# Row-sum reciprocals and scalings moved to later steps in the 256-query blocks of a transformer layer, and one output product of the tail moved

## The chip, the cores and the metric

The kernel runs on one core of a Trainium2 chip. The metric is the device time of one launch in microseconds (us), the median of several runs. Lower is better.

## What is computed

A pre-norm transformer layer on one sequence of 2048 tokens with 512 features: attention with 32 heads of 16 features, and then a gated feed-forward part with 1792 inner features. Inputs are bf16.

```python
def _A_ref(x, wqkv, wo):                       # S=2048, D=512, H=32, Dh=16
    qkv = ((x @ wqkv).reshape(B, S, 3, H, Dh)).transpose(2, 0, 3, 1, 4)
    q, k, v = qkv[0], qkv[1], qkv[2]
    p = softmax(einsum("bhqd,bhkd->bhqk", q, k) * Dh ** -0.5)
    o = einsum("bhqk,bhkd->bhqd", p, v)
    return o.transpose(0, 2, 1, 3).reshape(B, S, D) @ wo
def _B_ref(x, w_gate, w_up, w_down):           # F=1792
    h = sigmoid(x @ w_gate) * (x @ w_up)
    return h @ w_down
h = x + _A_ref(_layernorm(x), A_wqkv, A_wo)
h2 = h + _B_ref(_layernorm(h), B_w_gate, B_w_up, B_w_down)
```

## The kernel before

**Tiling.** The queries are cut into five chunks (`CHUNKS`): three of 512 queries and, at the end, two of 256 (chunks 3 and 4). Within a chunk, the 32 heads are worked on in eight groups of four. One pair (chunk, head group) is called a block here and written (c, g). There are 39 blocks with a normalization of their own through DRAM, and 15 of these have 256 queries: (3, 0) to (3, 7) and (4, 0) to (4, 6). The last one, (4, 7), is normalized in the tail in another way.

**Steps.** Everything after a prologue is one list of 683 steps, written out by a loop over `i`. A step holds three score tiles of 128 keys by 512 columns. `emit_scores` writes the score products on TensorE (L937, with dummy products L914 at some steps) into one of two score buffers `pss`, and the exponentials of ScalarE (L948), which read them. At every fourth step (`i % 4 == 0`), and at a few more, the third tile is left to VectorE instead, which computes the exponential in pieces: `exp_bits` (L967) in the step itself, `exp_first` (L970 and L973) one step later, `exp_second` (L976) two steps later and `exp_third` (L980) three steps later. L967 is what reads the score buffer, so it sets it free for the scores two steps on.

The products with V (L1020, `emit_pv`) are planned by `plan_pv`: those of four steps are done six steps after the first of the four. With the last one of a block, at a step that I call the block's step i, `emit_norm` starts the normalization:

- VectorE copies the sums and unnormalized outputs out of `acc` (L993, `xs_all`). SyncE's queue (SP) writes the four rows of sums to DRAM (four issues, L996, `sd`) and reads them back spread over partitions (L997, `s_all`).
- `recip`, at a later step: VectorE's reciprocal (L1004, `r_all`), SP's write to DRAM (L1006, `rd`) and four broadcast reads (L1008, `rb_all`).
- `scale`, at a still later step: VectorE multiplies `xs_all` by `rb_all` into `OT` (L1000), which the output product reads (L630, `wo_mm`).

**Order in a step.** The engines run their instructions in the order in which the program writes them. A step is written in this order: the scores and exponentials with the loads of the Q rows of the next block (L246) and of its bounds (L256) on SP if they are due; the V products with `emit_norm`; what `later` put down for this step, in the order in which it was put down; and then the fill. The fill (`emit_fill`) takes work of other kinds from a generator: for the chunk before, the output product and layer norm (L630, L639, L147 to L158, transposes L164 and L165, loads of x with L635), the gate and up products (L655) with the tanh on ScalarE (L660) and the product on VectorE (`up_mul`, L668), and the down products (L671, L676, and the store L678). These products share one PSUM buffer `pm`: the next one can start only when the last one was read. At some steps the fill comes ahead of the V products or of what is due.

**The steps of a block's normalization.** A 256-query block ends at a step i with `i % 4 == 2`. Before the change, `recip` is due at i+6 and `scale` at i+11, except in (3, 7) and (4, 6), where they are due at i+5 and i+10.

**Tail.** `wo_early` writes the first output products of the last chunk's first 128 rows (head groups 0 to 6) as fill; the one of group 6 is held back until all steps are done. `ffn_last` then normalizes the last block with products on TensorE (L798 for the sums, L802, L805 and L806, L808), does the rest of the output products, and the feed-forward part of the last chunk.

Of the kernel before, what the change touches and what calls it, by code (L numbers as in the profile page):

```python
# [20 lines left out]
def kernel(  # L21
# [19 lines left out]
    NG = H // 4  # L41
    FC = F // P
    QC = 512
    TQ = QC // P
    CHUNKS = [(0, QC), (QC, QC), (2 * QC, QC), (3 * QC, QC // 2), (3 * QC + QC // 2, QC // 2)]
    NC = len(CHUNKS)
# [26 lines left out]
    def pm_tile():  # L73
        return pmh["pool"].tile([P, 512], FP32, name="pm")
# [424 lines left out]
    NS = len(groups)  # L499
# [124 lines left out]
    def tiles_of(c):  # L624
        q0, w = CHUNKS[c]
        return range(q0 // P, (q0 + w) // P)

    def wo_mm(ps, c, tt, g):
        assert ("o", c, g) in ready
        nc.tensor.matmul(ps[:], lhsT=OT[c % 2][:, g, tt * P:(tt + 1) * P], rhs=wo_pad[:, g, :],  # L630
                         start=(g == 0), stop=(g == NG - 1))

    def x_load(t):
        xr = pmh.get("work", work).tile([P, D], BF16, name="xr")
        nc.sync.dma_start(out=xr[:], in_=x_v[:, t, :])  # L635
        return xr
# [132 lines left out]
    def wo_early(c):  # L769
        early["x"] = [x_load(t) for t in tiles_of(c)]  # L770
        early[0] = pm_tile()
        for g in range(NG - 1):
            if g == NG - 2:
                for _ in range(3):
                    yield ("from", NS + LAG)
            yield 1
            wo_mm(early[0], c, 0, g)

    def ffn_last(c):
        q0, w = CHUNKS[c]  # L780
# [6 lines left out]
        def wo(tt, g0, g1):  # L787
            for g in range(g0, g1):
                wo_mm(pss[tt], c, tt, g)

        def add_x(tt):
            nc.tensor.matmul(pss[tt][:], lhsT=ident_bf[:], rhs=xrs[tt][:], start=False, stop=False)
# [16 lines left out]
                             rhs=ident_f[:], start=True, stop=True)  # L809
        nc.vector.tensor_tensor(out=OT[c % 2][:, NG - 1, 0:w], in0=xs, in1=rb[:, 0:w], op=ALU.mult)  # L810
        ready.add(("o", c, NG - 1))
        wo(1, 6, NG - 1)
        add_x(0)
        add_x(1)
# [57 lines left out]
    def filler():  # L872
        for t in range(NV0, NT):
            yield from fill_v(t)
        yield from fill_k(1, True)
        for b in range(2, 4):
            yield from fill_k(b)
            yield from fill_q0(b)
        for qc in range(1, NQC):
            yield from fill_q(qc)  # L880
        for c in range(NC - 1):
            yield ("from", int(first_step(c + 1)) + (11 if c + 3 >= NC else 15))
            yield from ffn_tasks(c)
        yield from wo_early(NC - 1)
# [98 lines left out]
    def norm_part(t, w, n):  # L983
        k = t.shape[1] * w // QC
        o = k * (n % (QC // w))
        return t[:, o:o + k]

    def emit_norm(c, g, i):
        w = CHUNKS[c][1]
        b = w // 32  # L990
        wait = int(w < QC and g < NG - 1 - (c == NC - 1))
        xs, rb, s32, r32 = (norm_part(t, w, g) for t in (xs_all, rb_all, s32_all, r32_all))
        nc.vector.tensor_copy(out=xs, in_=acc[:, 0:w])  # L993
        sd = dram.tile([4, w], FP32, name="sd", tag="sd%d" % w)
        for j in range(4):
            nc.sync.dma_start(out=sd[j:j + 1, :], in_=xs[32 * j + DH:32 * j + DH + 1, :])  # L996
        nc.sync.dma_start(out=s32, in_=sd[:].rearrange("j (a b) -> (j a) b", b=b))  # L997

        def scale():
            nc.vector.tensor_tensor(out=OT[c % 2][:, g, 0:w], in0=xs, in1=rb, op=ALU.mult)  # L1000
            ready.add(("o", c, g))

        def recip():
            nc.vector.reciprocal(out=r32, in_=s32)  # L1004
            rd = dram.tile([4, w], FP32, name="rd", tag="rd%d" % w)
            nc.sync.dma_start(out=rd[:].rearrange("j (a b) -> (j a) b", b=b), in_=r32)  # L1006
            for j in range(4):
                nc.sync.dma_start(out=rb[32 * j:32 * j + 32, :], in_=rd[j:j + 1, :].to_broadcast([32, w]))  # L1008
            later(i + 10 + wait, scale)
        later(i + 5 + wait, recip)  # L1010

    def emit_pv(c, g, k, i):
# [16 lines left out]
    def later(i, fn):  # L1029
        due.setdefault(i, []).append(fn)  # L1030

    p_of = {}
    fl = filler()
    state = {"turn": False, "wait": 0, "debt": 0.0, "done": False, "next": 0, "rate": None}

    def emit_fill(i):
        state["step"] = i
        r = rate(i)
        if not r or state["done"] or i < state["wait"]:
            state["debt"] = 0.0  # L1040
            return
        state["debt"] += state["rate"] or r
        while state["debt"] > 0 or isinstance(state["next"], tuple):
            c = state["next"]
            state["next"] = next(fl, None)
            if c is None:
                state["done"] = True
                return
            if isinstance(c, tuple):
                kind, n = c  # L1050
                if kind == "rate":
                    state["rate"] = n
                    continue
                state["debt"] = 0.0
                state["wait"] = i + 1 + n if kind == "gap" else i + 1 + (n - i - 1) % CYC if kind == "at" else n
                return
            state["debt"] -= c
            made[i] += c
# [11 lines left out]
    def load_w():  # L1070
        steps = [(wg[:, c, :], wg_v[:, c, :]) for c in range(DC)]
        steps += [(wu[:, c, :], wu_v[:, c, :]) for c in range(DC)]
        for k, (o, i) in enumerate(steps):
            later(44 + 5 * k, lambda o=o, i=i: nc.sync.dma_start(out=o, in_=i))
        for f in (0, 7):
            later(GM + 21 + f // 2, lambda f=f: nc.sync.dma_start(out=wd[:, f:f + 7, :], in_=wd_v[:, f:f + 7, :]))

    LAG = 2
# [10 lines left out]
    def plan_pv():  # L1089
        plan, last = {}, 0  # L1090
        for n, group in enumerate(groups):
            if n < G1:
                if n % CYC == 0:
                    last = n + CYC + 2
                    for k, u in enumerate(units[n * GU:(n + CYC) * GU:4]):
                        if k and u[2] == 0:
                            last += 1
                        plan.setdefault(last, []).append(u)
            else:
                for u in group:  # L1100
                    if u[3] == 3:
                        last = max(last, n + LAG)
                        plan.setdefault(last, []).append(u)
        return plan

    with tc.manual_schedule():
        p1ctx = ExitStack()
        pmh["pool"] = p1ctx.enter_context(tc.tile_pool(name="ps_p1", bufs=6, space=PSUM))
        prologue(p1ctx.enter_context(tc.tile_pool(name="pro", bufs=1)))
        p1ctx.close()  # L1110
        pmh["pool"] = ps_misc
        sctx = ExitStack()
        ps_s = sctx.enter_context(tc.tile_pool(name="ps_s", bufs=1, space=PSUM))
        ptp = sctx.enter_context(tc.tile_pool(name="ptp", bufs=1))
        pss2 = [ps_s.tile([P, GU, QC], FP32, name=f"pss{k}") for k in range(2)]
        pt4 = [ptp.tile([P, GU, QC], BF16, name=f"pt{k}") for k in range(4)]
        later(12, clear_wo)
        later(72, load_wo)
        later(90, lambda: nc.gpsimd.tensor_copy(out=ident_f[:], in_=ident_bf[:]))
        load_w()  # L1120
        pv_due = plan_pv()
        n_pv = {i: len(us) if i < G1 + CYC else 0 for i, us in pv_due.items()}
        for i in range(NS + LAG):
            if i < NS:
                emit_scores(i)
            if i == NS + LAG - 1:
                while next(fl) == 1:
                    pass
            us = pv_due.pop(i, [])
            early_fill = i >= 2 * CYC and any(u[2] == 0 for u in us)  # L1130
            for u in us:
                if early_fill and u[2] == 0:
                    emit_fill(i)
                emit_pv(*u[:3], i)
            if state["turn"] and i == state["wait"] and not early_fill:
                emit_fill(i)
                early_fill = True
            for fn in due.pop(i, []):
                fn()
            if 1 <= i < NS and not early_fill:  # L1140
                emit_fill(i)
        for _ in fl:
            pass
        sctx.close()
        pmh["pool"] = ctx.enter_context(tc.tile_pool(name="ps_t", bufs=6, space=PSUM))
        pmh["work"] = ctx.enter_context(tc.tile_pool(name="tail", bufs=4))
        assert not due
        ffn_last(NC - 1)


# [28 lines left out]
```

## Time and profile before

| | us |
|---|---|
| median of 3 runs | 951.39 |
| lowest and highest of these | 951.03 and 952.76 |
| the profiled execution, device time | 954.82 |
| its span from the first to the last instruction | 952.1 |
| TensorE (PE) busy in it | 848.2 |
| ScalarE (ACT) busy | 897.1 |
| VectorE (DVE) busy | 781.1 |
| GpSimd (POOL) busy | 32.3 |

The views of the profile are of the one profiled execution. Busy times are sums over the whole span; what a wait costs has to be read in the stage in which it occurs. In the timeline's rows the first two numbers are start and duration in us, and a bracket at the end tells the idle time of the engine before the instruction and what ended it. SPq is SyncE's queue, which issues nearly all the DMAs. In a row of windows each engine has its busy time and, in parentheses, its number of instructions; the three numbers at the end are the granted share of the TensorE clock, the DMA share and GB/s.

### The profile page before, as it was taken

How to read it: one execution, taken by the hardware profiler on the slowest of the kernel's cores; microseconds unless marked ns; L12 is line 12 of the kernel's file. 1: busy time of each engine (PE TensorE's matmuls, PEld its weight loads, DVE VectorE, ACT ScalarE, POOL GpSimd, SP SyncE). 2: the span in 40 equal slices, each digit the busy share in tenths (PEclk: the TensorE clock that was granted, in tenths of full speed). 3: DMA queues.
4: the chain of work that ended last, by engine and by line, in shares of the span. 5: the costliest groups of instructions: out<-in, count | busy, mean ns of one | idle time of the engine just before them, and what ended most of it. 6: DMA issues, size and time to landing. Idle time of an engine off the chain costs nothing.

```text
span 952.1 us, 17365 instructions
## 1 busy us (share of the span) xinstructions
PE 848.2 (89%) x6474; PEld 341.6 (36%) x6474; DVE 781.1 (82%) x1413; ACT 897.1 (94%) x778; POOL 32.3 (3%) x52
## 2 busy tenths in 40 slices
PE   5998888888899999988888999888888999988998
PEld 3322222222232222222222223222355555556656
DVE  8589988878788888899888888889898688778743
ACT  6999999999999999999999999999999999999962
POOL 5300000000000000000000000000000000000000
PEclk9999999999999999999999999999999999999999
DMA  5202450000002000000010000000010000010010
GB/s 162 47 2 59 124 129 16 16 16 16 21 20 92 15 16 17 22 26 23 2 27 27 15 16 16 21 8 27 16 32 21 16 11 16 27 28 21 10 29 18
DMA packets 38381, 29.50 MB, mean 31 GB/s; under 512 B 17884, under 2 KB 33528, under 8 KB 38296
## 3 DMA queue, kind: packets, MB, share of 16 engines
q1 hardware_dynamic: 38152, 28.27, 11.4%
q8 instruction: 50, 0.82, 0.4%
q14 instruction: 35, 0.29, 0.1%
q10 hardware_dynamic: 144, 0.13, 0.1%
HBM read 20.31 MB, written 2.61 MB: 24 GB/s over the span
## 4 chain that ended last, share of the span: by engine, by line
PE 43%; ACT 25%; DVE 22%; issue 6%; DMA 2%; SPq 1%; POOL 0%; ACTq 0%; DVEq 0%
PE pss L937 21%; ACT pt L948 14%; PE acc L1020 8%; PE pm L655 6%; ACT wd L948 4%; ACT stg L948 4%; DVE stg L967 3%; PE pm L671 2%; ACT QTu L948 2%; DVE y L976 2%; DVE pt L980 2%; DVE y L973 2%; DVE reg L970 2%; PE pm L173 1%; DVE reg L668 1%
## 5 line engine op out<-in xcount | busy, mean ns | idle before, releaser
L937 PE MATMUL pss<-QB,KT 128*128 128x512 bf16 (+3 forms) x2554 | 477.9, 337 | 54.8 <-ACT pt L948 26.1
L948 ACT ACTIVATE pt<-pss 128x1536 bf16<-128x1536 f32 (+1 forms) x392 | 501.0, 1358 | 11.1 <-PE pss L937 6.8
L937 PEld LDWEIGHTS <-KT 64*128 64x128 bf16 (+1 forms) x2554 | 179.4, 95 | 322.8 <-issue 209.0
L948 ACT ACTIVATE stg<-pss 128x1536 bf16<-128x1536 f32 (+1 forms) x140 | 182.6, 1352 | 4.7 <-PE pss L937 3.4
L967 DVE TENSOR_SCALAR stg<-pss 128x512 int32<-128x512 f32 x123 | 84.8, 689 | 65.4 <-PE pss L937 54.7
L1020 PE MATMUL acc<-pt,Vaug 128*17 128x512 bf16 (+1 forms) x1471 | 112.6, 338 | 3.3 <-DVE xs_all L993 1.6
L948 ACT ACTIVATE wd<-pss 128x1536 bf16<-128x1536 f32 (+1 forms) x80 | 103.6, 1383 | 0.2
L948 ACT ACTIVATE QTu<-pss 128x1024 bf16<-128x1024 f32 (+1 forms) x71 | 95.2, 1341 | 2.3 <-PE pss L937 1.9
L973 DVE SCALAR_TENSOR_TENSOR y<-reg 128x512 f32<-128x512 f32 x123 | 85.2, 692 | 4.2
L976 DVE SCALAR_TENSOR_TENSOR y<-y,reg 128x512 f32<-128x512 f32 x123 | 84.3, 685 | 1.4
L1020 PEld LDWEIGHTS <-Vaug 128*17 128x17 bf16 x2560 | 49.5, 89 | 96.9 <-issue 82.5
L655 PE MATMUL pm<-reg,reg 128*128 128x512 bf16 (+1 forms) x280 | 58.0, 337 | 8.2 <-DVE reg L668 8.1
L655 PE MATMUL pm<-reg,wu 128*128 128x512 bf16 (+1 forms) x280 | 58.1, 338 | 1.1 <-ACT sg L660 1.1
L671 PE MATMUL pm<-wd,reg 128*128 128x512 bf16 x196 | 54.9, 382 | 0.6 <-DVE ob L676 0.6
L970 DVE TENSOR_SCALAR reg<-stg 128x512 int32<-128x512 int32 x123 | 51.7, 421 | 1.5
L1020 PE MATMUL acc<-stg,Vaug 128*17 128x256 bf16 (+1 forms) x564 | 50.6, 326 | 0.3 <-DVE stg L980 0.2
L980 DVE SCALAR_TENSOR_TENSOR pt<-y,stg 128x512 bf16<-128x512 f32 x70 | 48.0, 686 | 1.9
L668 DVE SCALAR_TENSOR_TENSOR reg<-sg,pm 128x512 bf16<-128x512 f32 x56 | 38.2, 683 | 11.1 <-PE pm L655 10.7
L967 DVE TENSOR_SCALAR wd<-pss 128x512 int32<-128x512 f32 x45 | 31.0, 689 | 18.7 <-PE pss L937 17.5
L660 ACT ACTIVATE sg<-pm 128x512 f32<-128x512 f32 x56 | 35.4, 632 | 10.3 <-PE pm L655 10.2
L154 POOL TENSOR_TENSOR rs<-ve,pw_neg 128x1 f32<-128x1 f32 x16 | 11.1, 696 | 880.9 <-DVE ve L152 880.9
L173 PE MATMUL pm<-reg 128*128 128x512 bf16 x124 | 37.5, 397 | 0.1
(153 smaller groups left out, 726.8 us busy)
## 6 DMA issues: line engine op xcount, KB each, us to landing
rb_all<-rd SPq DMA_DIRECT2D x96, 64.0 KB
xr<-in_A_x_dram SPq DMA_DIRECT2D x16, 128.0 KB
out_dram<-ob SPq DMA_DIRECT2D x15, 128.0 KB
rb_all<-rd SPq DMA_DIRECT2D x60, 32.0 KB
reg<-in_A_x_dram SPq DMA_DIRECT2D x7, 256.0 KB
KT<-stg SPq DMA_DIRECT2D x7, 256.0 KB
reg<-in_B_w_gate_dram SPq DMA_DIRECT2D x4, 448.0 KB
wu<-in_B_w_up_dram SPq DMA_DIRECT2D x4, 448.0 KB
```

The source lines that it names most:

```text
L173: nc.tensor.matmul(ps[:], lhsT=wqkv_sb[:, c, w0:w0 + P], rhs=xnT[:, c, n * QC:(n + 1) * QC], start=(c == 0), stop=(c == DC - 1))
L655: nc.tensor.matmul(ps[:, i * w:(i + 1) * w], lhsT=wt[:, c, f * P:(f + 1) * P], rhs=hnT[:, c, 0:w], start=(c == 0), stop=(c == DC - 1))
L668: nc.vector.scalar_tensor_tensor(out=out, in0=a, scalar=1.0, in1=b, op0=ALU.add, op1=ALU.mult)
L671: nc.tensor.matmul(ps[:], lhsT=hT[:, f, tt * P:(tt + 1) * P], rhs=wd[:, f, :], start=(f == 0), stop=(f == FC - 1))
L937: nc.tensor.matmul(pss[:, ui, h * w:(h + 1) * w], lhsT=KT[rows, g, kt * P:(kt + 1) * P], rhs=QB[n_qg % 2][rows, j, 0:w], start=True, stop= ...
L948: ex = nc.scalar.activation(out=pt[:, 0:na, :], in_=pss[:, 0:na, :], func=ACT.Exp, scale=DH ** -0.5 / QS)
L967: return nc.vector.tensor_scalar(out=e_bits, in0=src, scalar1=ONE_BITS, scalar2=0.0, op0=ALU.add, op1=ALU.max)
L970: nc.vector.tensor_scalar(out=e_man, in0=e_bits, scalar1=0x7FFFFF, scalar2=-0x40800000, op0=ALU.bitwise_and, op1=ALU.bitwise_or)
L973: nc.vector.scalar_tensor_tensor(out=e_pol, in0=m, scalar=PA, in1=m, op0=ALU.add, op1=ALU.mult)
L976: nc.vector.scalar_tensor_tensor(out=e_pol, in0=e_pol, scalar=PB, in1=e_man.bitcast(FP32), op0=ALU.add, op1=ALU.mult)
L980: nc.vector.scalar_tensor_tensor(out=dst, in0=e_pol, scalar=PC, in1=e_bits.bitcast(FP32), op0=ALU.add, op1=ALU.mult)
L1020: nc.tensor.matmul(acc[32 * j:32 * j + VW, 0:w], lhsT=Vaug[:, kt, 4 * g + j, :], rhs=p[:, h * w:(h + 1) * w], start=(kt == 0), stop=(kt == ...
```

## The change

In the 256-query blocks (3, 0) to (3, 6) and (4, 0) to (4, 5), `recip` is now due at i+7 instead of i+6, and `scale` at i+13 instead of i+11. In (3, 7), `recip` moves from i+5 to i+7 and `scale` from i+10 to i+13. In (4, 6) both stay at i+5 and i+10. In the tail, the output product of head group 6 for the first 128 rows is written after the scaling of the last block, beside that of the second 128 rows, instead of ahead of the sums.

```diff
     def wo_early(c):
         early["x"] = [x_load(t) for t in tiles_of(c)]
         early[0] = pm_tile()
-        for g in range(NG - 1):
-            if g == NG - 2:
-                for _ in range(3):
-                    yield ("from", NS + LAG)
+        for g in range(NG - 2):
             yield 1
             wo_mm(early[0], c, 0, g)
 
@@ ffn_last
         nc.vector.tensor_tensor(out=OT[c % 2][:, NG - 1, 0:w], in0=xs, in1=rb[:, 0:w], op=ALU.mult)
         ready.add(("o", c, NG - 1))
+        wo(0, 6, NG - 1)
         wo(1, 6, NG - 1)
         add_x(0)
         add_x(1)
@@ emit_norm
-        wait = int(w < QC and g < NG - 1 - (c == NC - 1))
+        wait = 2 * int(w < QC and (c < NC - 1 or g < NG - 2))
...
-            later(i + 10 + wait, scale)
+            later(i + 10 + wait + wait // 2, scale)
         later(i + 5 + wait, recip)
@@ the loop over steps
             if i == NS + LAG - 1:
-                while next(fl) == 1:
+                while next(fl, None) == 1:
                     pass
```

## The prediction

> **What bounds the kernel now.** I read the page's busy times first, then the list of waits, then the stretch of the 256-query blocks (700 to 920 us) by windows and by the timelines of VectorE, TensorE, ScalarE and SP.
>
> ```profile
> span 952.1 us, 17365 instructions
> PE 848.2 (89%) x6474; PEld 341.6 (36%) x6474; DVE 781.1 (82%) x1413; ACT 897.1 (94%) x778; POOL 32.3 (3%) x52
> ```
>
> ScalarE is the fullest engine, so a wait elsewhere costs only what of it reaches ScalarE. The change moves two of VectorE's instructions, and both wait for DMAs. Here are their rows in the list of waits between 698 and 924 us (total, times, longest), and the long ones in VectorE's timeline:
>
> ```profile
> DVE OT L1000 <- DMA rb_all<-rd: 11.9, 5, 5.4
> DVE r_all L1004 <- DMA s_all<-sd: 2.2, 2, 1.2
> ...
> 733.54 0.42 DVE L1000 TENSOR_TENSOR OT<-xs_all,rb_all 128x256 bf16<-128x256 f32 x1 [1.55 <-DMA rb_all<-rd]
> 737.45 0.69 DVE L967 TENSOR_SCALAR stg<-pss 128x512 int32<-128x512 f32 x1 [0.50 <-PE pss L937]
> 739.38 0.20 DVE L1004 RECIPROCAL r_all<-s_all 128x8 f32<-128x8 f32 x1 [1.24 <-DMA s_all<-sd]
> 745.55 0.43 DVE L1000 TENSOR_TENSOR OT<-xs_all,rb_all 128x256 bf16<-128x256 f32 x1 [1.83 <-DMA rb_all<-rd]
> 850.17 0.43 DVE L1000 TENSOR_TENSOR OT<-xs_all,rb_all 128x256 bf16<-128x256 f32 x1 [2.77 <-DMA rb_all<-rd]
> 920.51 0.42 DVE L1000 TENSOR_TENSOR OT<-xs_all,rb_all 128x256 bf16<-128x256 f32 x1 [5.44 <-DMA rb_all<-rd]
> ```
>
> The last, 5.44 us, is block (4, 6), whose steps do not change. So 11.9 - 5.4 = 6.5 us of waits at scalings can go: 1.55 in (3, 1), 1.83 in (3, 2), 2.77 in (4, 1) and a small rest. What do they cost? VectorE's queue behind a scaling holds L970, L973 and `up_mul` L668, and L668 frees the one `pm` buffer for TensorE's next gate product L655. In TensorE's and ScalarE's timelines, and then in two windows:
>
> ```profile
> 747.69 1.02 PE L655 MATMUL pm<-reg,reg 128*128 128x512 bf16 x4 [1.50 <-DVE reg L668]
> 748.75 0.60 ACT L660 ACTIVATE sg<-pm 128x512 f32<-128x512 f32 x1 [0.67 <-PE pm L655]
> 749.89 5.05 ACT L948 ACTIVATE pt<-pss 128x1024 bf16<-128x1024 f32 x4 [0.55 <-PE pss L937]
> 731.50:749.89 18.39, 15.56 (x172) 8.68 (x168) 11.97 (x22) 16.91 (x16) 0.00 (x0) 1.00 0.08 17
> 749.89:766.17 16.28, 15.72 (x172) 8.82 (x169) 11.81 (x22) 16.28 (x16) 0.00 (x0) 1.00 0.05 12
> ```
>
> The windows hold twelve steps each and equal work (172 products, 22 instructions on VectorE, 16 on ScalarE). In the second, ScalarE is never idle; the first, with the waits of (3, 1) and (3, 2), takes 18.39 - 16.28 = 2.11 us more. That is the prize in chunk 3.
>
> **Where the moved instructions go.** A block ends at a step 2 modulo 4. Its reciprocal goes from a step 0 modulo 4 to a step 1 modulo 4, where it was put down before `exp_first` and so stands just ahead of L970; before, it stood just behind L967. Between the two places lies only fill, no piece of an exponential, so its own wait of 1.24 does not go by this move; it goes only if `s_all` lands sooner. The scaling goes from just ahead of L970 to just ahead of L980, behind L970, L973, L668, L976 and the next block's L993:
>
> ```profile
> 745.89 0.42 DVE L970 TENSOR_SCALAR reg<-stg 128x512 int32<-128x512 int32 x1
> 746.35 0.69 DVE L973 SCALAR_TENSOR_TENSOR y<-reg 128x512 f32<-128x512 f32 x1
> 747.89 0.68 DVE L976 SCALAR_TENSOR_TENSOR y<-y,reg 128x512 f32<-128x512 f32 x1
> ```
>
> That gives the broadcast at least 0.42 + 0.69 + 0.68 = 1.79 us more to land, against waits of 1.55 and 1.83. What would still wait holds up L980 and the next L967, no longer L668. Nothing is added: a scaling stays one instruction of 0.42 us without DMAs, a reciprocal one of 0.20 with five issues on SP (L1006 and four L1008). POOL's queue is not touched.
>
> **SP's queue.** The five issues move past the loads of Q rows and bounds (L246, L256) in the four blocks where these are written at the reciprocal's new step: counting units, (3, 1), (3, 4), (3, 7) and (4, 2), at steps 545, 577, 609 and 641. The SP rows of (3, 1) before, and one from the start of chunk 3:
>
> ```profile
> 727.30 0.19 DVE L1004 RECIPROCAL r_all<-s_all 128x8 f32<-128x8 f32 x1
> 727.52 0.34 SPq L1006 DMA_DIRECT2D rd<-r_all  x1
> 728.98 2.73 SPq L1008 DMA_DIRECT2D rb_all<-rd  x4
> 731.75 2.46 SPq L246 DMA_DIRECT2D QB<-QTu  x4
> 735.61 1.23 SPq L996 DMA_DIRECT2D sd<-xs_all  x4
> 680.26 3.02 SPq L246 DMA_DIRECT2D QB<-QTu  x4
> 682.04 5.20 ACT L948 ACTIVATE pt<-pss 128x1536 bf16<-128x1536 f32 x4
> 727.01 1.48 ACT L948 ACTIVATE QTu<-pss 128x1536 bf16<-128x1536 f32 x1
> ```
>
> The loads take SP 735.61 - 731.75 = 3.86 us. Where nothing stands before them they leave early: those at 680.26 are written at step 513, whose exponential is the third of the four that begin at 682.04 (step 511), near 684.4. With the same 4 us of lead, those of step 545 (its exponential starts at 727.01) leave near 723 and are gone when the reciprocal is done. Bounds: the write of `rd` 0 to 3.86 us later; I take 0, by the row at 680.26. Then L996 of (3, 2), which waited behind them until 735.61, goes out some 3 us earlier, and the wait of 1.24 at 739.38 goes with it. So no wait of the stage is left, and I count the whole 2.11 (other bound: 0.67 + 0.55 = 1.22, ScalarE's two idle times alone).
>
> **Block (3, 7)** moves furthest, past two L967, an L676 and the loads:
>
> ```profile
> 815.77 0.36 SPq L678 DMA_DIRECT2D out_dram<-ob  x1
> 819.72 1.26 SPq L256 DMA_DIRECT2D QB<-bnd  x2
> 825.34 0.68 DVE L980 SCALAR_TENSOR_TENSOR pt<-y,stg 128x512 bf16<-128x512 f32 x1
> 843.53 0.37 SPq L1006 DMA_DIRECT2D rd<-r_all  x1
> 846.87 1.71 SPq L1008 DMA_DIRECT2D rb_all<-rd  x4
> ```
>
> Here a store (L678) holds the loads back, so the write leaves behind them, at 819.72 + 1.26 = 821.0. From write to first broadcast (3, 1) took 728.98 - 727.52 = 1.46, the four issues here would take 1.71, and from the last issue to the scaling (3, 1) took 733.54 - 731.71 = 1.83: `rb_all` comes at 826.0. The scaling stands just ahead of this L980, at about 825.0, because it no longer runs before it. So 1.0 us of wait at L980, while L676, which TensorE's down products wait for, runs 0.35 earlier. I take +0.1. If the write lands as slowly as in the last two rows, behind a store (846.87 - 843.53 = 3.34), it is 1.9 worse; bounds -0.3 to +1.9.
>
> **Block (4, 1)** has the longest wait, 2.77, and ScalarE's longest gap in these blocks follows it:
>
> ```profile
> 853.51 1.02 ACT L948 ACTIVATE QTu<-pss 128x1024 bf16<-128x1024 f32 x1 [1.70 <-PE pss L937]
> 852.46 0.39 SPq L635 DMA_DIRECT2D xr<-in_A_x_dram  x1
> 854.64 0.69 DVE L639 TENSOR_TENSOR reg<-pm,xr 128x512 f32<-128x512 f32 x1 [0.44 <-DMA xr<-in_A_x_dram]
> 859.45 0.69 DVE L967 TENSOR_SCALAR stg<-pss 128x512 int32<-128x512 f32 x1
> ```
>
> The scaling's wait goes, since it moves behind the copy L993 that TensorE needs. But VectorE then meets L639, and that waits for a load of x which SP issues at 852.46, behind L1008, L246 and L256 in an order that stays. L639 remains at 854.64, VectorE works without a break from there to L967 at 859.45, and TensorE needs that L967 for its scores. What is won at 850 is given back by 860: 0; the other bound is 1.70 won. The remaining blocks show waits below 1 us that ScalarE does not feel: 0.
>
> **The tail.** After the last scaling, VectorE copies and TensorE runs three output products and the sums; then a row of the chain and two windows:
>
> ```profile
> 920.86 0.42 DVE L795 COPY xs_all<-acc 128x256 f32<-128x256 f32 x1
> 920.99 0.82 PE L630 MATMUL pm<-wo_pad,OT 128*128 128x512 bf16 x3 [0.90 <-DVE OT L1000]
> 922.16 1.68 PE pm L630 x4
> 922.00:923.00 1.00, 1.00 (x5) 0.41 (x5) 0.43 (x2) 0.30 (x1) 0.00 (x0) 0.55 0.00 0
> 923.00:924.00 1.00, 1.00 (x4) 0.70 (x3) 0.00 (x0) 0.00 (x0) 0.00 (x0) 0.50 0.00 0
> ```
>
> The sums come at 920.99 + 0.82 = 921.8. With group 6 out of the way, the other two products run during the idle 0.90, and the sums wait for the copy alone, until 921.3: 0.5 earlier. The moved product comes back behind them, at 1.68 / 4 = 0.42. Net -0.1; other bounds +0.4 (nothing earlier) and the price of the clock below.
>
> From 922 on, the clock is granted at half, after gaps on TensorE of at most 0.90 us. With 0.5 less of idle time the halving might stay out, which is a rival below. The Trainium skill ("TensorE: Matmul & The Clock Gate", Part 1: The HAM clock gate) has the clock go to half only after an idle window of about 3.4 us. By that rule a gap of 0.9 or of 0.4 would change nothing and this rival would have no chance; the rows disagree with it, so the rival keeps one.
>
> **Sum.** -2.11 (chunk 3) + 0.1 (3, 7) + 0 (4, 1) - 0.1 (tail) = -2.1 us: for the profiled execution 954.82 - 2.1 = 952.7. That execution lies 3.4 above the median of the runs; for the median, 951.39 - 2.1 = 949.3. By the bounds of the first term and the better one of (3, 7) its own range is 948.8 to 950.2.
>
> **Rivals.** *Given back*: a later anchor eats the stage's gain, as in (4, 1); only the tail's 0.1 is left: 951.3. For it: VectorE paces the stretches with layer norms. Against: ScalarE is never idle from 749.89 to 766.17, so what it gains it keeps there. *More*: (4, 1) also keeps its 1.70: 947.6; L635 stands against it. *Full clock in the tail*: the rate stays whole; the halved stretch, some 3.4 us, is worth 1.7: 947.6. For it: one gap shrinks; against: another of some 0.4 to 0.7 opens while the copy is awaited. *Slower*: the loads of Q rows don't leave early, and in (3, 1) the broadcast comes 3.86 us later. The scaling then waits 1.55 + 3.86 - 1.79 = 3.6 at L980, 3.1 more than the 0.50 that L967 idles there; (3, 7) adds 1.9; of the prize only the 1.22 behind (3, 2) comes: 951.39 + 3.1 + 1.9 - 1.2 = 955.2. Half as late, (3, 1) costs 1.2 and (3, 7) 1.0: 952.4. It decides if `rd` of (3, 1) is written later than about 729.
>
> **Chances.** Forecast 0.52, given back 0.16, more 0.09, full clock 0.09, slower 0.14. A measurement can tell some 0.2%, 1.9 us, from no change, so faster means below 949.5: all of "more" and "full clock" and 0.29 of the forecast's 0.52, 0.47 in all. Slower than that 0.14; within, the remaining 0.39. The range goes from the two better rivals less 0.7, half the width of the forecast's own range, to a place between the half-late and the full slower case: 946.9 to 953.2. It leaves out both gains together and the worst of the slower case.
>
> **What would show it.** Right: no wait of L1000 for `rb_all` over 1 us before the last, which stays near 5.4; L655's waits for L668 between 730 and 750 gone; those twelve steps in about 16.3; L639's wait for `xr` in (4, 1) grown from 0.44 towards 2; the sums 0.5 earlier after the last scaling. Wrong: waits of over 1 us at L1000 or L1004 in (3, 1) or (3, 2), or twelve steps still at 18.

## The result, and the profile after

| | before | after |
|---|---|---|
| median, us | 952.02 (22 runs) | 950.09 (22 runs) |
| lowest and highest | 950.88 and 953.28 | 949.11 and 951.92 |
| ratio after to before | | 0.9981, 95% interval 0.9975 to 0.9988 |
| the profiled execution, device time | 954.82 | 949.8 |
| its span | 952.1 | 948.0 |

The changed kernel is faster by 1.9 us, about 0.2%; the interval of the ratio leaves out 1. The forecast was 2.1 less than before (951.39 to 949.3). On the chip of the last group of experiments the same kernel had a median of 949.58 us against 951.82, ratio 0.9977 (0.9968 to 0.9986).

In the changed kernel's program the lines are numbered two lower in the steps (L1000 is now L998, L1004 is L1002, L1006 is L1004, L1008 is L1006, L639 stays) and three lower in the tail (L798 is now L795, L802 is L799). The first two rows of its page:

```profile
span 948.0 us, 17271 instructions
PE 839.5 (89%) x6375; PEld 340.1 (36%) x6474; DVE 781.5 (82%) x1413; ACT 896.7 (95%) x778; POOL 32.4 (3%) x52
```

ScalarE's and VectorE's work is the same (896.7 and 781.5 us against 897.1 and 781.1). Only idle time went. TensorE's busy time is 8.7 us lower, but that shows no saving: its weight loads are as many as before (6474), while 99 records of matmuls are missing from this trace (6375 against 6474). The list of VectorE's waits between 694 and 922 us (total, times, longest):

```profile
DVE OT L998 <- DMA rb_all<-rd: 5.9, 2, 5.2
DVE reg L639 <- PE pss L935: 1.4, 1, 1.4
```

The scalings' waits for `rb_all` fell from 11.9 us in five to 5.9 in two, and 5.2 of that is block (4, 6), which was not to change. VectorE's timeline in (3, 1) and (3, 2), with SP's rows for (3, 1) and the gate product that used to wait 1.50:

```profile
733.16 0.68 DVE L668 SCALAR_TENSOR_TENSOR reg<-sg,pm 128x512 bf16<-128x512 f32 x1
727.69 0.19 DVE L1002 RECIPROCAL r_all<-s_all 128x8 f32<-128x8 f32 x1
734.36 0.42 DVE L998 TENSOR_TENSOR OT<-xs_all,rb_all 128x256 bf16<-128x256 f32 x1
737.13 0.19 DVE L1002 RECIPROCAL r_all<-s_all 128x8 f32<-128x8 f32 x1
745.90 0.42 DVE L998 TENSOR_TENSOR OT<-xs_all,rb_all 128x256 bf16<-128x256 f32 x1
723.43 2.90 SPq L246 DMA_DIRECT2D QB<-QTu  x4
727.91 0.35 SPq L1004 DMA_DIRECT2D rd<-r_all  x1
729.34 2.42 SPq L1006 DMA_DIRECT2D rb_all<-rd  x4
731.85 1.10 SPq L994 DMA_DIRECT2D sd<-xs_all  x4
745.42 0.82 PE L655 MATMUL pm<-reg,reg 128*128 128x512 bf16 x3
```

None of the scalings or reciprocals carries a bracket: they find their data there. The Q rows leave at 723.43, ahead of the reciprocal, so `rd` is written at 727.91, only 0.39 us after its old time of 727.52. The sums of (3, 2) go out at 731.85 instead of 735.61. `up_mul` (L668) runs ahead of the scaling, and L655 starts without idle time. The twelve steps 548 to 560 and the twelve after them, by windows:

```profile
731.56:747.67 16.11, 15.31 (x165) 8.69 (x167) 12.03 (x23) 16.11 (x16) 0.00 (x0) 1.00 0.07 18
747.67:764.17 16.50, 15.68 (x170) 8.86 (x170) 11.92 (x21) 16.50 (x16) 0.00 (x0) 1.00 0.05 12
```

The first stretch took 18.39 us before. ScalarE, the fourth busy time of the row, is busy for all of the 16.11 us. Against the old profile the stage gained 2.28 us.

Next (3, 7), (4, 1) and the tail, in the timelines of SP, VectorE, ScalarE and TensorE:

```profile
818.86 0.34 SPq L1004 DMA_DIRECT2D rd<-r_all  x1
823.53 0.42 DVE L998 TENSOR_TENSOR OT<-xs_all,rb_all 128x256 bf16<-128x256 f32 x1 [0.70 <-DMA rb_all<-rd]
850.12 1.02 ACT L946 ACTIVATE QTu<-pss 128x1024 bf16<-128x1024 f32 x1 [0.35 <-PE pss L935]
850.06 0.39 SPq L635 DMA_DIRECT2D xr<-in_A_x_dram  x1
852.24 0.69 DVE L639 TENSOR_TENSOR reg<-pm,xr 128x512 f32<-128x512 f32 x1 [1.43 <-PE pss L935]
858.38 0.38 PE L164 MATMUL pm<-ident_bf,xn 128*128 128x128 bf16 x4 [1.71 <-DVE reg L639]
859.46 1.45 ACT L946 ACTIVATE stg<-pss 128x1536 bf16<-128x1536 f32 x1 [1.24 <-DVE ve L152]
917.99 0.43 DVE L998 TENSOR_TENSOR OT<-xs_all,rb_all 128x256 bf16<-128x256 f32 x1 [5.19 <-DMA rb_all<-rd]
918.33 0.42 DVE L792 COPY xs_all<-acc 128x256 f32<-128x256 f32 x1
918.89 0.58 PE L795 MATMUL pm<-ident_f,xs_all 128*128 128x4 f32 x4 [0.71 <-DVE xs_all L792]
919.58 0.21 DVE L799 RECIPROCAL r<-pm 128x8 f32<-128x8 f32 x1 [0.83 <-PE pm L795]
```

In (3, 7) the scaling still waits, 0.70 us. In (4, 1) ScalarE's gap of 1.70 shrank to 0.35, but L639 now waits 1.43, and nine microseconds later ScalarE has a gap of 1.24 where it had 0.32. The bracket of L639 names TensorE (L935), but L639 starts 2.18 us after its load L635 was issued (852.24 - 850.06), just as before (854.64 - 852.46), so the load is what it waits for; an experiment below shows it. What ties these two together is the row of TensorE: the transposes L164 stand ahead of the scores in its order, and they wait 1.71 us for `pm`, which the second L639 reads late. In the tail the sums (L795) wait for the copy (L792) alone.

The spans differ by 4.1 us, more than the medians. The difference has a second part, in the clock. Before's profile had 0.55 and 0.50 of the clock around 923 us; after's has all of it there:

```profile
920.00:922.00 2.00, 2.00 (x13) 1.18 (x12) 0.54 (x3) 0.12 (x1) 0.00 (x0) 1.00 0.00 0
922.00:924.00 2.00, 2.00 (x11) 0.92 (x10) 1.90 (x7) 0.00 (x0) 0.54 (x1) 1.00 0.00 0
```

By the profiles alone, then, two accounts fit: the waits in chunk 3, and the tail's clock, which the prediction had as a rival.

### The profile page after: what moved, and what is told of

The parts are those of the page before. It is cut to its first block, busy times and chain, and to the rows that moved or that the text cites. A ratio compares the mean times of both kernels' runs of the same rounds, so it can differ in the third digit from the quotient of the medians.

```text
span 948.0 us, 17271 instructions
## 1 busy us (share of the span) xinstructions
PE 839.5 (89%) x6375; PEld 340.1 (36%) x6474; DVE 781.5 (82%) x1413; ACT 896.7 (95%) x778; POOL 32.4 (3%) x52
## 4 chain that ended last, share of the span: by engine, by line
PE 43%; ACT 25%; DVE 23%; issue 6%; DMA 1%; POOL 0%; SPq 0%; ACTq 0%; DVEq 0%
PE pss L935 21%; ACT pt L946 15%; PE acc L1018 8%; PE pm L655 6%; ACT stg L946 4%; ACT wd L946 4%; DVE stg L965 3%; ACT QTu L946 2%; PE pm L671 2%; DVE y L974 2%; DVE pt L978 2%; DVE reg L968 1%; PE pm L173 1%; DVE y L971 1%; PE pm L630 1%
## 5 line engine op out<-in xcount | busy, mean ns | idle before, releaser
L935 PE MATMUL pss<-QB,KT 64*128 64x512 bf16 (+3 forms) x2526 | 474.3, 337 | 58.0 <-ACT pt L946 26.4
L935 PEld LDWEIGHTS <-KT 64*128 64x128 bf16 (+1 forms) x2554 | 179.3, 95 | 324.6 <-issue 209.9
L655 PE MATMUL pm<-reg,reg 128*128 128x512 bf16 (+1 forms) x262 | 56.9, 335 | 6.2 <-DVE reg L668 5.3
L655 PE MATMUL pm<-reg,wu 128*128 128x512 bf16 (+1 forms) x271 | 57.6, 337 | 1.7 <-ACT sg L660 1.2
L671 PE MATMUL pm<-wd,reg 128*128 128x512 bf16 x175 | 51.6, 382 | 2.4 <-issue 1.3
L668 DVE SCALAR_TENSOR_TENSOR reg<-sg,pm 128x512 bf16<-128x512 f32 x56 | 38.3, 684 | 11.1 <-PE pm L655 10.7
```

Source lines behind the costliest of these rows:

```text
L655: nc.tensor.matmul(ps[:, i * w:(i + 1) * w], lhsT=wt[:, c, f * P:(f + 1) * P], rhs=hnT[:, c, 0:w], start=(c == 0), stop=(c == DC - 1))
L668: nc.vector.scalar_tensor_tensor(out=out, in0=a, scalar=1.0, in1=b, op0=ALU.add, op1=ALU.mult)
L671: nc.tensor.matmul(ps[:], lhsT=hT[:, f, tt * P:(tt + 1) * P], rhs=wd[:, f, :], start=(f == 0), stop=(f == FC - 1))
L935: nc.tensor.matmul(pss[:, ui, h * w:(h + 1) * w], lhsT=KT[rows, g, kt * P:(kt + 1) * P], rhs=QB[n_qg % 2][rows, j, 0:w], start=True, stop= ...
```

## The experiments

The ratios below are against the kernel before, run in turn with the experiments on one chip; there were three groups (before: 951.72, 951.56 and 951.82 us).

### The two halves, and the kernel before again

The steps alone (e1_steps) and the tail alone (e2_tail), put on the kernel before:

```diff
-        wait = int(w < QC and g < NG - 1 - (c == NC - 1))
+        wait = 2 * int(w < QC and (c < NC - 1 or g < NG - 2))
...
-            later(i + 10 + wait, scale)
+            later(i + 10 + wait + wait // 2, scale)
```

```diff
-        for g in range(NG - 1):
...
+        for g in range(NG - 2):
             yield 1
...
+        wo(0, 6, NG - 1)
         wo(1, 6, NG - 1)
```

> The kernel before, unchanged, as a control. Two theories are to be told apart in this group of runs. 'Waits': the time comes from the two blocks (3, 1) and (3, 2), whose waits cost 2.2 us between steps 548 and 560, and the tail moves by 0.1. 'Tail clock': the step gains are given back, and the time comes from TensorE's clock, which is halved for some 3.4 us in the tail before and not after; that would be worth 1.7. Both expect a ratio of 1.000 here, within 0.001. 'Tail clock' expects a mean granted clock of 0.998 in nearly all runs of this kernel (the profiled execution after has 1.000); 'waits' makes no claim on it.

> The reciprocals and scalings moved as in the change, the tail as before. 'Waits' expects 2.0 to 2.3 us less than before, about 949.9, nearly all of the change. 'Tail clock' expects no more than 0.5 us, and the granted clock as in the kernel before.

> Only the tail's product of group 6 moved, all steps as before. 'Waits' expects -0.1 us, a ratio of 1.000. 'Tail clock' expects -1.5 to -1.9 us with a granted clock of 1.000 in most runs.

Measured: before again 951.81 us, ratio 0.9996 (0.9987 to 1.0004); the steps alone 949.84, ratio 0.9977 (0.9967 to 0.9987); the tail alone 951.89, ratio 0.9999 (0.9990 to 1.0008). The whole gain belongs to the steps. 'Tail clock' expected a mean clock of 0.998 in nearly all runs of the kernel before; all 11 runs of the control had 1.000. Here are, of the control's profile, the stretches 548 to 560 and (4, 1), steps 632 to 648, and the place in the tail where the first profile had half the clock; after them the same two stretches of the tail alone:

```profile
731.61:749.76 18.15, 15.58 (x172) 8.69 (x168) 11.98 (x23) 16.82 (x17) 0.00 (x0) 1.00 0.07 17
846.63:869.30 22.67, 19.66 (x231) 12.22 (x231) 18.61 (x38) 20.86 (x18) 1.18 (x2) 1.00 0.12 29
922.00:924.00 2.00, 2.00 (x13) 0.92 (x12) 1.12 (x2) 0.00 (x0) 0.00 (x0) 1.00 0.00 0
```

```profile
731.43:748.96 17.53, 15.57 (x172) 8.68 (x168) 11.97 (x22) 16.78 (x16) 0.00 (x0) 1.00 0.07 18
845.79:869.04 23.25, 19.66 (x231) 12.23 (x231) 18.61 (x38) 20.86 (x18) 1.15 (x2) 1.00 0.11 28
```

Both executions had the full clock throughout, with the old tail and with the new one (mean 1.000). And the steps alone had the clock halved in another place, at 860 us:

```profile
858.00:860.00 2.00, 1.81 (x34) 1.28 (x33) 1.90 (x7) 0.73 (x1) 0.25 (x1) 0.89 0.00 1
860.00:862.00 2.00, 2.00 (x18) 1.01 (x11) 1.97 (x5) 1.38 (x2) 0.41 (x1) 0.50 0.05 6
```

So whether the clock is halved, and where, differs from execution to execution of one kernel. Of the 22 runs of the changed kernel, 5 had a mean clock of 0.998 and a median of 951.15 us, and 17 had 1.000 and 949.80: a halving costs about 1.4 us there. The rival "full clock in the tail" falls: the tail edit alone changes nothing, and the gain stands among runs with the full clock alone (on the last group's chip 951.75 us before, 19 runs, and 949.58 for the changed kernel, 10 runs).

The rows also price the first term anew. The stage with the old steps took 18.39, 18.15 and 17.53 us in three executions, 18.02 in the mean, and 16.11 to 16.13 in six executions with the new steps: 1.9 us, where the one profile gave 2.28.

### Only blocks (3, 1) and (3, 2)

```diff
         wait = int(w < QC and g < NG - 1 - (c == NC - 1))
+        late = (c, g) in ((3, 1), (3, 2))
...
-            later(i + 10 + wait, scale)
-        later(i + 5 + wait, recip)
+            later(i + 10 + wait + 2 * late, scale)
+        later(i + 5 + wait + late, recip)
```

> Only the two blocks (3, 1) and (3, 2) have their reciprocal one step and their scaling two steps later; everything else is as before. 'Waits' expects the same as for all fourteen blocks: -2.0 to -2.3 us, twelve steps from 548 to 560 in 16.1 to 16.5 instead of 18.4. If the other twelve blocks bring something, this one is slower than the kernel with all steps moved by that much; 'tail clock' expects no change.

Measured: 949.89 us, ratio 0.9975 (0.9965 to 0.9985), the same as the steps in all blocks (949.84). Its stage and its (4, 1), which has the old steps here:

```profile
731.46:747.59 16.13, 15.58 (x170) 8.70 (x167) 12.00 (x23) 16.13 (x17) 0.00 (x0) 1.00 0.08 17
844.67:867.90 23.23, 19.66 (x231) 12.23 (x231) 18.62 (x38) 20.87 (x18) 1.18 (x2) 1.00 0.11 28
```

Two of the fourteen blocks whose steps move give all of the gain; the other twelve add up to about nothing.

### The scalings alone, the reciprocals alone

The scalings at i+13 with the reciprocals where they were (e4_scale), and the reciprocals at i+7 with the scalings where they were (e5_recip):

```diff
+        late = 2 * int(w < QC and (c < NC - 1 or g < NG - 2))
...
-            later(i + 10 + wait, scale)
+            later(i + (10 if not late else 13), scale)
```

```diff
-        later(i + 5 + wait, recip)
+        later(i + 5 + max(wait, late), recip)
```

> Only the scalings are moved, to the step of the change; the reciprocals stay at their old steps, and the tail is as before. Theory 'both moves': in (3, 1) the scaling no longer waits, but on SP the Q rows still stand ahead of the sums of (3, 2), so the reciprocal of (3, 2) waits some 2 us for its sums where it waited 1.24, and the first two cycles of the stage (548 to 556) win at most 0.2; only the 1.4 of the third cycle (556 to 560) come, so -1.2 to -1.5 us. Theory 'scaling alone': the wait at the scaling is all that costs, and the whole -1.9 comes.

> Only the reciprocals are moved, to the step of the change; the scalings stay at their old steps, so one step fewer lies between the two. 'Both moves': the scaling of (3, 1) waits as long as before (some 1.5 us), that of (3, 2) some 0.6 instead of 1.8, since its sums come earlier; -0.5 to -1.0 us. 'Scaling alone': the reciprocal's step brings nothing, the scalings wait longer by some tenths, 0 to +0.5 us.

Measured: the scalings alone 950.19 us, ratio 0.9992 (0.9983 to 1.0001), an interval that just takes in no change; the reciprocals alone 956.68, ratio 1.0056 (1.0043 to 1.0068). By the medians the scalings alone gain 1.4 us, as 'both moves' expected, by the ratio 0.8. Their waits in the stage are gone, but the reciprocal of (3, 2) now takes up the waiting, as this list shows, and the stage takes 17.04 instead of 16.11. (In this profile the bracket of L639 names the load of x.)

```profile
DVE r_all L1005 <- DMA s_all<-sd: 3.1, 2, 2.4
DVE reg L639 <- DMA xr<-in_A_x_dram: 1.4, 1, 1.4
731.55:748.59 17.04, 15.32 (x168) 8.64 (x169) 11.97 (x23) 16.51 (x17) 0.00 (x0) 1.00 0.08 20
```

So the scaling's step gives about half of the stage's gain (18.02 - 17.04 = 1.0), and the other half needs the reciprocal's, through SP's queue: only when the reciprocal is a step later do the Q rows leave ahead of it, and the next block's sums in time.

With the reciprocals alone, the one of (3, 2) no longer waits, and the scaling of (3, 1) still waits 1.45 us; the stage takes 16.62. The kernel's loss was foreseen by neither theory. It stands in one place, (3, 7), in the rows of SP, VectorE and TensorE and in windows:

```profile
819.18 0.34 SPq L1007 DMA_DIRECT2D rd<-r_all  x1
823.85 0.42 DVE L1001 TENSOR_TENSOR OT<-xs_all,rb_all 128x256 bf16<-128x256 f32 x1 [4.24 <-DMA rb_all<-rd]
825.65 0.61 PE L1021 MATMUL acc<-pt,Vaug 128*17 128x256 bf16 x8 [4.41 <-DVE pt L980]
824.00:826.00 2.00, 0.34 (x8) 0.12 (x7) 1.93 (x5) 0.00 (x0) 0.00 (x0) 0.89 0.04 3
826.00:828.00 2.00, 2.00 (x17) 0.72 (x10) 1.36 (x2) 0.68 (x1) 0.00 (x0) 0.50 0.00 0
818.19:834.71 16.52, 12.00 (x112) 6.40 (x114) 9.35 (x18) 10.48 (x10) 0.00 (x0) 0.90 0.09 26
```

There the reciprocal is two steps later (i+7 instead of i+5), `rd` leaves behind the store and the Q rows at 819.18, and the scaling is still at i+10: it waits 4.24 us, TensorE stands for 4.41 us, and then runs at half clock for a while; steps 612 to 620 (the last row) take 16.52 us. To test that this one block was the whole loss, it alone was put back (the lines below are against the reciprocals alone):

```diff
-        late = 2 * int(w < QC and (c < NC - 1 or g < NG - 2))
+        late = 2 * int(w < QC and (c < NC - 1 or g < NG - 2) and (c, g) != (3, NG - 1))
```

> The reciprocals one step later and the scalings where they were, as in the experiment that took 5.1 us more, but with block (3, 7) left as before. Theory 'the whole loss was (3, 7), whose broadcast is issued behind the store and the Q rows while its scaling waits at i+10': no loss between steps 608 and 616, the gain of 1.8 at step 560 kept, the median 1.4 to 1.9 below the kernel before. Rival 'later reciprocals cost in the other blocks as well, since the scalings stand where they stood': twelve steps gain, but chunk 4's blocks (4, 1) to (4, 4) lose, and the median is within 0.5 of before or above it.

Measured: 950.56 us, ratio 0.9981 (0.9972 to 0.9990). Steps 612 to 620 take 11.10 us, as in the kernel before (11.10), and the stage of (3, 1) takes 17.06:

```profile
731.51:748.57 17.06, 15.38 (x169) 8.74 (x168) 11.94 (x23) 16.52 (x16) 0.00 (x0) 1.00 0.07 17
818.57:829.67 11.10, 10.65 (x112) 5.91 (x114) 9.17 (x18) 10.37 (x9) 0.00 (x0) 1.00 0.10 27
```

The theory of (3, 7) holds: the loss is gone. The gain is 1.3 us by the medians, just under the 1.4 to 1.9 expected, and 1.8 by the ratio. In the stage the reciprocals alone get 1.0 of the 1.9 here (18.02 - 17.06), not the 1.8 that was expected; with (3, 7) moved too that stage, which the edit leaves as it is, took 16.62, so the split is known to some 0.4 us.

### The load that gives (4, 1)'s gain back

If L639's wait for `xr` is what gives the gain of (4, 1) back, then issuing that load early, in the fill of the chunk before, must keep it. On the changed kernel:

```diff
         for tt, t in enumerate(tiles_of(c)):
-            xr = x_load(t)
+            xr = early.pop("next", None) or x_load(t)
...
+            if c == NC - 3 and tt == len(tiles) - 1:
+                early["next"] = x_load(tiles_of(c + 1)[0])
```

> The changed kernel, with one more edit: the first load of x for chunk 3's layer norm is issued some ten steps earlier, with the last down products of chunk 2. Theory 'anchor': in (4, 1) what the scaling's later step wins (1.35 us between steps 632 and 636 in the changed kernel's profile) is given back because VectorE then waits for this load (1.43). With the load early, about 1 us of it stays: -0.9 to -1.3 against the changed kernel, so about -3 against before. Rival: the layer norm's chain on VectorE itself takes the time, and the gain is below 0.3.

> The changed kernel with the load of x for chunk 3's rows issued early, once more, as the yardstick for the store held back: the wait of L639 in (4, 1) gone, ratio 0.996 to 0.998, 1.3 to 1.9 us below the changed kernel on this chip.

Measured: 948.31 us, ratio 0.9969 (0.9957 to 0.9980), and on the other chip 948.35, ratio 0.9962 (0.9950 to 0.9975), against the changed kernel's 949.58 there. This version beats both kernels: on that chip its five runs all lie below the changed kernel's ten, and it is 1.2 us less by the medians, a little under the 1.3 to 1.9 expected. Of its second profile, L639 in (4, 1) and the stretch 632 to 648:

```profile
850.60 0.69 DVE L639 TENSOR_TENSOR reg<-pm,xr 128x512 f32<-128x512 f32 x1
844.37:866.22 21.85, 19.38 (x229) 12.15 (x231) 18.62 (x38) 20.80 (x19) 1.24 (x2) 1.00 0.09 24
```

L639 no longer waits. The stretch took 23.43 us in the changed kernel on that chip, so this is 1.58 less (1.31 less than the 23.16 of the changed kernel's first profile); the prediction's other bound for (4, 1) was 1.70.

### The last scaling's wait

The wait of 5.2 us at the scaling of (4, 6) is the longest left. The reciprocal's write and its first broadcast lie 2.48 and 2.72 us apart there in the changed kernel's two profiles, against 729.34 - 727.91 = 1.43 in (3, 1). Two tries to clear SP's queue ahead of them, the first on the changed kernel (the last chunk's loads of x behind the broadcasts), the second on top of the early load (the same, and the store of chunk 3's first rows held until step 680):

```diff
     def wo_early(c):
-        early["x"] = [x_load(t) for t in tiles_of(c)]
...
-        xrs = early["x"]
+        xrs = [x_load(t) for t in ts]
```

```diff
-        nc.sync.dma_start(out=out_v[:, t, :], in_=ob[:])
+        store = lambda: nc.sync.dma_start(out=out_v[:, t, :], in_=ob[:])
+        if hold:
+            later(hold, store)
+        else:
+            store()
...
-            down_out(psd, t, tt)
+            down_out(psd, t, tt, 680 if c == NC - 2 else None)
```

> The changed kernel, with one more edit: the two loads of x for the last chunk are issued after all steps, behind the broadcasts of block (4, 6), instead of ahead of its write of reciprocals. Theory 'queue': that write took 2.46 to 2.80 us to land because 256 KB of x stand before it, against 1.46 elsewhere; without them it takes 1.5 to 1.9, and the last scaling, which VectorE and TensorE wait 5.2 us for, comes 0.6 to 1.0 earlier: -0.6 to -1.0 us against the changed kernel. Rival: the store L678, which stays ahead, is what delays it; then 0, or up to +0.5 if the loads come too late for the tail's sums with x.

> The changed kernel with three edits in SyncE's queue: the load of x for chunk 3's rows is issued while the steps of chunk 3 run (as in the experiment that gave 948.31 us, ratio 0.9969), the last chunk's loads of x go behind the broadcasts of block (4, 6), and the store of the first output rows of chunk 3 is held back to step 680, so that no bulk transfer is under way when rd of (4, 6) is written. Theory 'the small write lands late behind bulk transfers': from write to first broadcast about 1.5 us as in (3, 1) instead of 2.2 to 2.5, the last scaling 0.7 to 1.0 earlier, the median 0.7 to 1.0 below the early load alone, near 947.5 us. Rival 'that time is the latency of a write and a read in a row': the last scaling where it was, the median within 0.3 of the early load alone.

> The changed kernel once more, beside the others on one chip: ratio near 0.998 (0.997 to 0.999), and twelve steps of the stage of (3, 1) and (3, 2) in 16.0 to 16.3 us. It is the control for the other three.

Measured: the loads late 950.03 us, ratio 0.9982 (0.9974 to 0.9991), where 0.6 to 1.0 us less than the changed kernel was expected and its ratio is no better than the changed kernel's 0.9981; the store held too 948.73, ratio 0.9969 (0.9958 to 0.9981), no better than the early load alone (948.35); the changed kernel 949.58, ratio 0.9977 (0.9968 to 0.9986), with the twelve steps in 16.11 us. SP's and VectorE's rows with the queue clear, and then SP's in the changed kernel:

```profile
910.96 0.34 SPq L1010 DMA_DIRECT2D rd<-r_all  x1
913.44 1.71 SPq L1012 DMA_DIRECT2D rb_all<-rd  x4
916.80 0.42 DVE L1004 TENSOR_TENSOR OT<-xs_all,rb_all 128x256 bf16<-128x256 f32 x1 [5.31 <-DMA rb_all<-rd]
```

```profile
912.46 0.33 SPq L1004 DMA_DIRECT2D rd<-r_all  x1
915.18 1.72 SPq L1006 DMA_DIRECT2D rb_all<-rd  x4
```

From write to read it is 2.48 us with nothing of bulk ahead of it, when the DMAs move 8 GB/s in that time, and 2.72 with it, at 46 GB/s; in the changed kernel's first profile it is 2.48 at 53 GB/s. The last scaling still waits 5.31. For (4, 6) the theory of bulk transfers falls. What makes this pair slower than that of (3, 1) stays open.

## Why the prediction was right

**Chunk 3: -2.11 forecast, right in mechanism.** It was 2.28 by the two profiles and 1.9 over the executions. The size of the prize came from one execution, and the same stage of the same kernel differs by 0.9 us between executions (18.39 to 17.53), so that 2.11 lies so near is in part luck. Two blocks alone give the whole median. ScalarE is not idle in the stage, and the waits of L655 are gone.

**SP's queue: 0 taken, 0.39 measured** (bounds 0 to 3.86). The Q rows left at 723.43, as worked out from the row at 680.26. That was the hinge of the rival "slower", which needed `rd` to be written after 729; it left at 727.91. The experiment with the scalings alone shows what the prediction only asserted: that the wait of 1.24 at the reciprocal goes through the earlier L996, and would otherwise grow (to 2.4).

**(3, 7): +0.1 forecast, about +0.1 measured.** Steps 612 to 620 took 11.10 us with the old steps, in four executions. With the new steps they took 11.40 and 11.37 in the two profiles of the changed kernel, and 11.05 to 11.36 in five more executions with other edits elsewhere, 11.24 in the mean of the seven. `rd` left at 818.86 (821.0 was worked out, in a profile that was 2.3 us later at that place), and the scaling waited 0.70 where 1.0 was expected. From the write to the first broadcast it took 1.42 us (820.28 - 818.86), close to the 1.46 that the prediction took, and not the 3.34 of its worse bound. With the scaling alone moved the stretch took 10.76, 0.34 less, close to the prediction's better bound of 0.3; with the reciprocal alone it took 16.52, 5.4 us more than before: the reciprocal must not move without its scaling.

**(4, 1): 0 forecast, 0 to +0.2 measured.** 23.17 us on average over four executions with the old steps (23.52 in before's first profile, 22.67, 23.25, 23.23), and with the new ones 23.16 and 23.43 in the two of the changed kernel and 23.53 with the last chunk's loads late. The gain came and was given back as the prediction said, with L639 waiting 1.43, and the early load shows the cause. One link was wrong: what TensorE waited for is not L967 in the first place but `pm` at the transposes L164, which the second L639 frees.

**Tail: -0.1 forecast, 0.0 measured.** The sums came 0.90 us after the scaling's start (918.89 - 917.99) instead of 1.14 (921.65 - 920.51): 0.24 earlier, not 0.5. The failed step compared the end of the three products (921.8) with the end of the copy, but the sums' row starts at 921.65, before those end. From the scaling's start to the reciprocal L799 it is 1.59 us (919.58 - 917.99) against 1.75 (922.26 - 920.51), and from there to the end 28.44 (948.02 - 919.58) against 28.25 in the second profile of the kernel before, with the full clock (921.11 to 949.36): 0.16 won, 0.19 given back.

**The sum.** -1.9 + 0.1 + 0.1 + 0.0 = -1.7 us by these terms, where -2.1 was forecast; the medians say -1.9, the interval of the ratio -1.1 to -2.4, and on the last group's chip the medians say -2.2. By the terms, chunk 3 was forecast 0.2 us too large, and the tail and (4, 1) 0.1 each. Why the medians lie nearer to the forecast than the terms do stays open. One possible reason is that the two later executions of the old stage (18.15 and 17.53 us) were faster than most: they took 951.14 and 950.95 us, where the medians of their kernels are 951.81 and 951.89, so their mean may price the stage too low.

**The clock.** The prediction gave the full clock in the tail 0.09, as if the halving belonged to the kernel's tail. After's profile showed just what that rival forecast, and the experiments refuted it. The profiled execution of before lay 3.4 us above the median partly because it was one of those with a halving.

## What to carry to other kernels

Before moving a step of a chain through DRAM, read the whole chain's queue: here the later reciprocal let other loads leave ahead of it and so brought the next block's sums sooner, and it did harm only where its reader stayed behind. Where a gain is given back by the next anchor, look what that anchor waits for: one load issued earlier was worth another 1.2 us, over half of this change. Do not price a stage from one profiled execution when the runs differ by as much as the gain, and do not take a difference in the clock for an effect of the edit until the unchanged kernel has been profiled again.

## What the hardware showed

The granted clock went to half in some executions of a kernel and not in others, and in different places: at 923 us in before's first profile, behind gaps of TensorE of 0.52 and 0.90 us, and at 860 in the steps alone, behind one of 1.95 us; the changed kernel's gap of 1.71 us in the same place had no halving. With the gap of 4.41 us in the reciprocals alone the clock fell to half, and all five runs of that kernel had a mean clock below 1. The Trainium skill ("TensorE: Matmul & The Clock Gate", Part 1: The HAM clock gate) gives a free-running window of about 3.4 us, idle for the clock to halve. The gap of 4.41 us agrees with that, and a window that runs free would fit a halving that comes and goes between executions; the gaps of 0.9 to 1.95 us, which are far shorter than such a window, do not fit an idle one.

The size of the gap goes with how often the clock is halved. In four kernels (the changed one, the steps alone, the scalings alone and the last chunk's loads late) TensorE's gap at the transposes L164 in (4, 1) is 1.70 to 2.08 us in the profiles, and 14 of their 62 runs had a mean clock below 1. In the others, the reciprocals alone left out, that gap is 0.40 to 0.80 us, and 7 of 128 runs had such a clock. Only one of the 14 has a profile that shows where the clock fell (the steps alone, just behind this gap), so that the gap is the cause is not shown.

The write of the reciprocals and the first broadcast lie 1.39 to 1.46 us apart in thirteen of the fifteen 256-query blocks of before's first profile, but 3.34 us in (4, 1) and 2.81 in (4, 6); in (4, 6) it is 2.2 to 2.8 us over ten profiles, with and without loads and a store ahead of them.
